# Two visits of small products made one: scores and sums of a head pair as one block inside an MLP unit

## The chip, the cores and the metric

The kernel runs on one core of one Trainium2 chip. The metric is the device time of one execution in microseconds; the kernel before takes 1026.38 us (median of three runs, 1025.25 to 1026.70). The five engines of the core are called as the profile calls them: PE is TensorE (PEld its weight loads), DVE is VectorE, ACT is ScalarE, POOL is GpSimd, SP is SyncE, which here only issues transfers.

## The reference

Retention (attention with a decay in place of a softmax), followed by an MLP with a PReLU. All of it is float32; `rel` is the distance of the positions, row minus column. Eight batches of eight heads, 576 positions, head dimension 64; the MLP has 4608 tokens, model width 512 and hidden width 2048.

```python
scores = scale * np.matmul(q, k.transpose(0, 1, 3, 2))      
gamma = 1.0 - 2.0 ** (-5.0 - np.arange(H, dtype=np.float32))
Dmat = np.where(rel >= 0, gamma[:, None, None] ** rel[None, :, :], 0.0)
attn_out = np.matmul(scores * Dmat[None, :, :, :], v)
x = attn_out.transpose(0, 2, 1, 3).reshape(B * S, H * D)
h = x @ w_in
g = np.maximum(h, 0.0) + alpha * np.minimum(h, 0.0)
out = g @ w_out
```

## The kernel before, in words

**Attention.** The kernel works on pairs of heads: number n of `pairs` is batch n // 4, heads 2c and 2c+1 with c = n % 4. The 576 positions are nine chunks (j) of 64. Inside a chunk the masked product of scores and values is computed directly. What earlier chunks give is carried in a running sum of 64x64 matrices. A pair goes through these steps:

- `load_pair`: twelve transfers bring kx and qx (blocks of 32 for the transposes), kn and vn. Two buffers of each, so a pair can be loaded while the one before it is in use.
- `scale_pair`: GpSimd multiplies qx by a table (L524), ScalarE scales vn by the decay (L529).
- `transposes`: VectorE turns qx and kx into qT and kT (L535). There is one buffer of each, and the running sums su share the buffer of kT.
- `pair_scores`: 18 products of 64x64 on TensorE (L552) into two PSUM tiles, even and odd chunks; ScalarE copies qT into mt (L555); four VectorE instructions scale and mask the scores into mt (L560).
- `pair_states`: 16 products of 64x64 (L571) into two PSUM tiles of the same pool (`ps_a`, two banks); ScalarE copies the even ones to su (L576), seven VectorE instructions form the running sums (L578, L582, L584). `pair_sums`: ScalarE copies them behind the values in vn (L590).
- `pair_values`: 18 products 128 deep and 64 wide (L601), and copies into the block of MLP input xb (L610).

A 64x64 product uses a quarter of the array[...]. The two heads and the even and odd chunks are laid out so that four products in a row use the four quarters.

**MLP.** Tokens go in 18 blocks (kb) of 256. From block 2 on each layer is a seven-product scheme in place of eight (sums of inputs and weights are made beforehand: `combine_x` on GpSimd, L449). A block is eight units (i). `mlp_unit` makes 14 products of the first layer (L463) into two PSUM tiles ph[0] and ph[1], one buffer each; ph[0] has four slots of 128 columns, of which three are used. ScalarE copies one slot (L469); VectorE adds the others (L474), applies the PReLU (L477, L479) and makes the sums for the second layer (L485), in the tile g. Then `mlp_out` makes the 14 records, seven products, of the second layer (L381) for the unit **before** this one, whose g is ready by then. With a block's last unit, seven VectorE instructions and two transfers write the output (L367, L368, L371).

**What sets the order.** Batches 0 and 1 and the first two token blocks are written out by hand. After `ordered.close()` a scheduler of the framework orders each engine's instructions from the order of the program and its own costs; each engine then runs them strictly in that order, and semaphores hold it where data is missing. The loop at L892 feeds it: for each pair of batches 2 to 7 (24 pairs) it writes the scores, then a third of the pair's share of MLP units, then the sums, a third, then the scaling and transposing of the next pair and the values, and the last third. A batch has 16 units to share out (24 for batch 4). 24 more units follow the last pair.

Of the kernel before, what the change touches and what calls it, by code (L numbers as in the profile page):

```python
# [18 lines left out]
def kernel(  # L19
# [49 lines left out]
    def half(x):  # L69
        return slice(x * C, (x + 1) * C)  # L70
# [36 lines left out]
    def load_pair(n):  # L107
        b, c = pairs[n]
        kx, qx, kn = [nat.tile([P, S], FP32, tag=t, name=f"{t}_{n}") for t in ("kx", "qx", "kn")]
        kx, qx = [t.rearrange("p (n r) -> p n r", r=32) for t in (kx, qx)]  # L110
        kn = kn.rearrange("p (j d) -> p j d", d=D)
        vn = nat.tile([P, 2, NJ, D], FP32, tag="vn", name=f"vn_{n}")
        load_sq(kx, k, b, c)
        load_sq(qx, q, b, c)
        for t, src in ((vn, v), (kn, k)):
            for h2 in range(2):
                load_head(t[half(1 - h2), h2] if t is vn else t[half(1 - h2)], src, b, 2 * c + h2)
        for h2 in range(2):

            nc.scalar.copy(vn[half(h2), h2, 0], zero[half(h2)])  # L120
        return kn, kx, qx, vn
# [326 lines left out]
                          (t[:, 2], b21, t[:, 1])):  # L448
            nc.gpsimd.tensor_tensor(out=o, in0=x0, in1=x1, op=ALU.subtract)  # L449

    def mlp_unit(kb, i):
        if kb not in xt:
            combine_x(kb)
        x, t = xb[kb], xt[kb]
        ph = [ps_h.tile([P, 4, P], FP32, tag=f"psh{m}", name=f"ph{m}_{kb}_{i}")
              for m in range(2)]

        for n, (m, o, l, r) in enumerate((
                (0, 2, 0, x[:, 0:2, 0:P]), (0, 0, 2, x[:, 2:4, 0:P]), (0, 1, 5, t[:, 1]),
                (1, 0, 4, t[:, 0]), (1, 1, 1, x[:, 0:2, P:TB]),  # L460
                (1, 2, 6, x[:, 2:4, P:TB]), (1, 3, 3, t[:, 2]))):
            for cc in range(2):
                nc.tensor.matmul(ph[m][:, o], w_in[i // UST][:, l, i % UST, cc], r[:, cc],  # L463
                                 start=(n in (0, 3) and cc == 0), stop=(n in (2, 6) and cc == 1),
                                 skip_group_check=True)


        g = mlp.tile([P, 8, P], FP32, tag="g", name=f"g_{kb}_{i}")
        nc.scalar.copy(g[:, 7], ph[0][:, 2])  # L469
        for o, x0, x1 in ((g[:, 0:5:4], ph[0][:, 0:2], g[:, 7:8].to_broadcast([P, 2, P])),  # L470
                          (g[:, 5:7], ph[1][:, 0:2], g[:, 4:5].to_broadcast([P, 2, P])),
                          (g[:, 3], ph[1][:, 0], g[:, 6]),
                          (g[:, 1:3], ph[1][:, 2:4], g[:, 5:7])):
            nc.vector.tensor_tensor(out=o, in0=x0, in1=x1, op=ALU.add)  # L474
        for m in range(2):
            fc = m * NU + i
            nc.vector.tensor_scalar(g[:, 4 + 2 * m:6 + 2 * m], g[:, 2 * m:2 * m + 2], 0.0,  # L477
                                    alpha[:, fc:fc + 1], ALU.min, ALU.mult)
        nc.vector.scalar_tensor_tensor(  # L479
            out=g[:, 0:4].rearrange("p x t -> p (x t)"),  # L480
            in0=g[:, 0:4].rearrange("p x t -> p (x t)"), scalar=0.0,
            in1=g[:, 4:8].rearrange("p x t -> p (x t)"), op0=ALU.max, op1=ALU.add)
        for o, x0, x1, op in ((4, 1, 3, ALU.add), (6, 0, 1, ALU.subtract),
                              (5, 4, 0, ALU.subtract), (7, 2, 5, ALU.subtract)):
            ins = nc.vector.tensor_tensor(out=g[:, o, :], in0=g[:, x0, :], in1=g[:, x1, :], op=op)  # L485

        combine(3, ins)
        assert i < NU - UST or not waiting
        pend.append((kb, i, g))
        if len(pend) > 1:  # L490
            mlp_out()
# [14 lines left out]
    def pop_units(n):  # L506
        for _ in range(min(n, len(queue))):
            kb, i = queue.pop(0)
            mlp_unit(kb, i)
            if i == NU // 2 and kb + 1 < NKB and ready[kb + 1] <= done[0]:  # L510
                combine_x(kb + 1)

# [30 lines left out]
    def pair_scores(n, kT, qT):  # L543
        c = pairs[n][1]

        mt = attn.tile([P, 2 * S], FP32, tag="at", name=f"mt_{n}").rearrange(
            "p (h j s) -> p h j s", h=2, s=C)
        ps = [ps_tile([P, NM, C], f"ps{p2}_{n}") for p2 in range(2)]
        for j in range(NJ):
            for h2 in range(2):  # L550
                x = (1 - h2, h2)[j % 2]
                nc.tensor.matmul(ps[j % 2][half(x), j // 2], kT[half(h2), chunk(j)],  # L552
                                 qT[half(h2), chunk(j)], start=True, stop=True)
        for h2 in range(2):
            nc.scalar.copy(mt[half(h2), h2].rearrange("p j s -> p (j s)"), qT[half(h2)])  # L555
        for p2 in range(2):
            for h2 in range(2):
                h, to, x = 2 * c + h2, half(1 - h2), (1 - h2, h2)[p2]
                nm = NM - p2
                nc.vector.scalar_tensor_tensor(  # L560
                    out=mt[to, h2, p2::2], in0=ps[p2][half(x), 0:nm], scalar=th[to, 3, h:h + 1],
                    in1=mask[to, None, :].to_broadcast([C, nm, C]), op0=ALU.mult, op1=ALU.mult)
        return mt

    def pair_states(n, kn, vn):
        c = pairs[n][1]
        ps = [ps_tile([P, NM - 1, D], f"pu{p2}_{n}") for p2 in range(2)]
        for j in range(NJ - 1):
            for h2 in range(2):
                x = (h2, 1 - h2)[j % 2]  # L570
                nc.tensor.matmul(ps[j % 2][half(x), j // 2], kn[half(1 - h2), j],  # L571
                                 vn[half(1 - h2), h2, j], start=True, stop=True)
        su = attn.tile([P, S], FP32, tag="kT", name=f"su_{n}")[:, 0:S - D].rearrange(
            "p (j d) -> p j d", d=D)
        g1, g2 = gch[:, 0, c:c + 1], gch[:, 1, c:c + 1]
        nc.scalar.copy(su[:, 0::2], ps[0])  # L576
        for h2 in range(2):
            nc.vector.scalar_tensor_tensor(  # L578
                out=su[half(h2), 1::2], in0=su[half(h2), 0::2], scalar=g1[half(h2)],
                in1=ps[1][half(1 - h2)], op0=ALU.mult, op1=ALU.add)  # L580
# [3 lines left out]
        nc.vector.scalar_tensor_tensor(out=su[:, 2::2], in0=su[:, 1:NJ - 3:2], scalar=g1,  # L584
                                       in1=ps[0][:, 1:], op0=ALU.mult, op1=ALU.add)
        return su

    def pair_sums(vn, su):
        for h2 in range(2):
            nc.scalar.copy(vn[half(h2), h2, 1:], su[half(h2)])  # L590

    def pair_values(n, vn, mt):
        b, c = pairs[n]
# [295 lines left out]
    enqueue(0)  # L889
    enqueue(1)  # L890

    for n, (b, c) in enumerate(pairs):  # L892
        if n <= last:
            continue
        if n == last + 1:
            pop_units(1)
        if n + 1 < len(pairs) and n + 1 not in loaded:
            loaded[n + 1] = load_pair(n + 1)
        kn, _, _, vn = loaded[n]
        share = -(-len(queue) // (NPAIR - c))  # L900
        cuts = [(share + i) // 3 for i in range(3)][::-1]
        kT, qT = turned.pop(n)
        mt = pair_scores(n, kT, qT)
        pop_units(cuts[0])
        pair_sums(vn, pair_states(n, kn, vn))
        pop_units(cuts[1])
        if n + 1 < len(pairs):
            scale_pair(n + 1)
            turned[n + 1] = transposes(n + 1)
        pair_values(n, vn, mt)  # L910
        del loaded[n]
        pop_units(cuts[2])
        if c == NPAIR - 1:
            enqueue(b)
    pop_units(len(queue))
    while pend:
        mlp_out()
# [28 lines left out]
```

## Time and profile before

| what | measured |
|---|---|
| time, median of three | 1026.38 us |
| span of the profiled execution | 1024.3 us |
| PE busy, matmuls | 1008.2 us, 98% |
| DVE busy | 767.9 us, 75% |
| ACT busy | 268.8 us, 26% |
| POOL busy | 179.0 us, 17% |
| granted PE clock | 0.995 |
| L381, second layer | 1792 records, 407.8 us busy |
| L463, first layer | 3584 records, 491.1 us busy in two groups |
| L552, L571, L601, attention | 1008, 896 and 1008 records, 22.3, 19.4 and 35.5 us busy |

Busy time is what the records cover. Matmuls are pipelined, so a record is longer than the distance to the next one: to price work on TensorE, subtract the starts of neighbouring groups in the timeline. A float32 product leaves two records. A bracket at the end of a timeline line is idle time of the engine ahead of it, with what ended it; a line without one started with no gap.

### The profile page before, as it was taken

To read this page: it belongs to the slowest core of one execution; us is meant where nothing else is said; L and a number is where in the kernel's file an instruction comes from. 1 tells how busy PE (TensorE), PEld (TensorE's weight loads), DVE (VectorE), ACT (ScalarE), POOL (GpSimd) and SP (SyncE) were. 2 spreads that over 40 slices of the span, in tenths; PEclk is the share of its full clock that TensorE was granted. 3 is DMA by queue.
4 is the path that set the end of the run, shared out by engine and by line. 5 is a ranking of instruction groups with operands and counts; after the bars stand their busy time and mean duration, and the time that the engine had idled before them with its cause. 6 is when DMAs were issued, how large, how long until landed. Compare 5 with 4: busy or idle time off the path is not lost.

```text
span 1024.3 us, 23109 instructions
## 1 busy us (share of the span) xinstructions
PE 1008.2 (98%) x9385; PEld 890.8 (87%) x9385; DVE 767.9 (75%) x2038; ACT 268.8 (26%) x605; POOL 179.0 (17%) x201
## 2 busy tenths in 40 slices
PE   6999999999999999999999999999999999999998
PEld 5666668999999999999999999999999999999997
DVE  6769967787878787776868787877787777667665
ACT  4656652223222222122122221222222211000000
POOL 5656675200200010100010000200020001010000
PEclk8999999999999999999999999999999999999999
DMA  9985744223223222112113222222222100000000
GB/s 238 235 195 150 180 78 93 48 57 59 64 41 68 48 47 57 25 46 47 39 30 67 48 53 45 63 48 56 48 48 57 24 22 2 22 1 21 1 21 22
DMA packets 229307, 64.30 MB, mean 63 GB/s; under 512 B 214336, under 2 KB 222544, under 8 KB 229200
## 3 DMA queue, kind: packets, MB, share of 16 engines
q1 hardware_dynamic: 227088, 62.29, 26.8%
q8 instruction: 74, 1.21, 0.5%
q10 hardware_dynamic: 2112, 0.53, 0.3%
q14 instruction: 33, 0.27, 0.1%
HBM read 53.35 MB, written 9.44 MB: 61 GB/s over the span
## 4 chain that ended last, share of the span: by engine, by line
PE 97%; SPq 1%; DVE 1%; ACT 0%; DMA 0%; issue 0%; DVEq 0%
PE ph L463 40%; PE po L381 38%; PE ph L419 6%; PE po L398 6%; PE pv L601 3%; PE ps L552 2%; PE pu L571 2%; SPq L78 1%; DMA raw<-in_moe_w_in_dram 0%; PE pv L720 0%; DVE wc L310 0%; DVE wc L307 0%; ACT wa L296 0%; ACT raw L298 0%; PE pv L709 0%
## 5 line engine op out<-in xcount | busy, mean ns | idle before, releaser
L381 PE MATMUL po<-w_out,g 128*128 128x256 f32 x1792 | 407.8, 379 | 0.0
L381 PEld LDWEIGHTS po<-w_out,g 128*128 128x128 f32 x1792 | 330.9, 190 | 39.6
L474 DVE TENSOR_TENSOR g<-ph,g 128x256 f32<-128x256 f32 (+1 forms) x512 | 187.9, 388 | 184.4 <-ACT g L469 112.6
L463 PE MATMUL ph<-xb,w_in 128*128 128x128 f32 x2048 | 277.7, 279 | 0.0
L463 PEld LDWEIGHTS ph<-xb,w_in 128*128 128x128 f32 x2048 | 253.2, 192 | 8.2 <-issue 0.5
L463 PE MATMUL ph<-xt,w_in 128*128 128x128 f32 x1536 | 213.4, 275 | 0.0
L463 PEld LDWEIGHTS ph<-xt,w_in 128*128 128x128 f32 x1536 | 192.1, 192 | 0.0
L469 ACT COPY g<-ph 128x128 f32<-128x128 f32 x128 | 33.9, 265 | 394.9 <-PE ph L463 372.9
L485 DVE TENSOR_TENSOR g<-g 128x128 f32<-128x128 f32 x512 | 126.9, 289 | 7.8
L479 DVE SCALAR_TENSOR_TENSOR g<-g 128x512 f32<-128x512 f32 x128 | 91.7, 717 | 3.9
L477 DVE TENSOR_SCALAR g<-g,alpha 128x256 f32<-128x256 f32 x256 | 85.0, 374 | 3.7
L524 POOL TENSOR_TENSOR qx<-qx,tabx 128x576 f32<-128x576 f32 x28 | 32.9, 1174 | 310.2 <-DMA qx<-in_q_dram 264.0
L419 PE MATMUL ph<-xb,w_in 128*128 128x256 f32 x256 | 61.1, 394 | 0.7 <-POOL w_out L697 0.7
L560 DVE SCALAR_TENSOR_TENSOR mt<-ps,th,mask 64x320 f32<-64x320 f32 (+1 forms) x112 | 57.8, 516 | 4.5 <-PE ps L552 2.6
L398 PE MATMUL po<-w_out,g 128*128 128x512 f32 x128 | 58.6, 599 | 0.9 <-DVE g L435 0.9
L419 PEld LDWEIGHTS ph<-xb,w_in 128*128 128x128 f32 x256 | 49.7, 197 | 10.7 <-issue 2.4
L449 POOL TENSOR_TENSOR xt<-xb 128x256 f32<-128x256 f32 x16 | 11.6, 727 | 214.6 <-PE ph L463 202.4
L449 POOL TENSOR_TENSOR xt<-xb,xt 128x256 f32<-128x256 f32 x32 | 23.6, 736 | 142.6 <-ACT xb L610 141.9
L529 ACT ACTIVATE vn<-vn,tabv 64x576 f32<-64x576 f32 x56 | 43.3, 773 | 16.7 <-DMA vn<-in_v_dram 15.9
L398 PEld LDWEIGHTS po<-w_out,g 128*128 128x128 f32 x128 | 23.4, 190 | 24.5 <-issue 21.8
L590 ACT COPY vn<-su 64x512 f32<-64x512 f32 x56 | 34.5, 616 | 37.8 <-DVE su L584 37.2
L610 ACT COPY xb<-pv 128x256 f32<-128x256 f32 (+3 forms) x84 | 22.6, 321 | 78.8 <-PE pv L601 78.7
(122 smaller groups left out, 688.5 us busy)
## 6 DMA issues: line engine op xcount, KB each, us to landing
out_dram<-osb SPq DMA_DIRECT2D x36, 256.0 KB, 2.3
kx<-in_k_dram SPq DMA_DIRECT2D x112, 72.0 KB, 2.7
qx<-in_q_dram SPq DMA_DIRECT2D x112, 72.0 KB, 2.4
vn<-in_v_dram SPq DMA_DIRECT2D x56, 144.0 KB, 3.2
kn<-in_k_dram SPq DMA_DIRECT2D x56, 144.0 KB, 3.2
raw<-in_moe_w_in_dram SPq DMA_DIRECT2D x24, 256.0 KB, 4.4
raw<-in_moe_w_out_dram SPq DMA_DIRECT2D x10, 512.0 KB, 5.2
w_in<-in_moe_w_out_dram SPq DMA_DIRECT2D x6, 512.0 KB, 5.1
```

Of the source, the lines that this page charges most:

```text
L381: nc.tensor.matmul(acc[kb][n // 2][:, n % 2, :], g[:, x, :], w_out[i][:, y, :], start=(i == 0 and n % 2 == 0), stop=(i == NU - 1 and (n % ...
L398: nc.tensor.matmul(acc[kb][m], g[:, 2 * x + m], w_out[i][:, 2 * x:2 * x + 2].rearrange("p x f -> p (x f)"), start=(i == 0 and x == 0), sto ...
L419: nc.tensor.matmul(ph[:, x], w_in[i // UST][:, cc // 2 * 2 + x, i % UST, cc % 2], xb[kb][:, cc], start=(cc == 0 and x == 0), stop=(cc == N ...
L449: nc.gpsimd.tensor_tensor(out=o, in0=x0, in1=x1, op=ALU.subtract)
L463: nc.tensor.matmul(ph[m][:, o], w_in[i // UST][:, l, i % UST, cc], r[:, cc], start=(n in (0, 3) and cc == 0), stop=(n in (2, 6) and cc == ...
L474: nc.vector.tensor_tensor(out=o, in0=x0, in1=x1, op=ALU.add)
L477: nc.vector.tensor_scalar(g[:, 4 + 2 * m:6 + 2 * m], g[:, 2 * m:2 * m + 2], 0.0, alpha[:, fc:fc + 1], ALU.min, ALU.mult)
L479: nc.vector.scalar_tensor_tensor(out=g[:, 0:4].rearrange("p x t -> p (x t)"), in0=g[:, 0:4].rearrange("p x t -> p (x t)"), scalar=0.0, in1 ...
L485: ins = nc.vector.tensor_tensor(out=g[:, o, :], in0=g[:, x0, :], in1=g[:, x1, :], op=op)
L529: nc.scalar.activation(vn[x, h2], vn[x, h2], ACTF.Copy, scale=tabv[x, c:c + 1])
L560: nc.vector.scalar_tensor_tensor(out=mt[to, h2, p2::2], in0=ps[p2][half(x), 0:nm], scalar=th[to, 3, h:h + 1], in1=mask[to, None, :].to_bro ...
L590: nc.scalar.copy(vn[half(h2), h2, 1:], su[half(h2)])
```

## The change

Before, TensorE leaves the MLP's 128x128 products three times for each pair: for the scores, the sums and the values, each between an L381 and an L463. After it, scores and sums are one block of 34 products of 64x64, placed inside a unit, behind its L463 products and ahead of L381. To have room for both in the two banks of `ps_a`, each tile now holds eight scores and eight sums, and the ninth score (chunk j=8) goes into the unused fourth slot of ph[0]. Its two small masks (64x64) are written directly behind the block, the four big ones after the unit's work on g, the running sums after the following unit, and the values with the next pair's scaling and transposes after the one behind that. The units that take a block are chosen so that none is a block's first or last unit: mostly the second and fifth.

```diff
-    def mlp_unit(kb, i):
+    def mlp_unit(kb, i, front=None):
...
+        rest = front(ph[0][:, 3]) if front else None
...
         combine(3, ins)
         assert i < NU - UST or not waiting
+        if rest:
+            rest()
         pend.append((kb, i, g))
...
+    def pair_front(n, kT, qT, kn, vn):
...
+        def products(extra):
+            ps = [ps_tile([P, 2, NM - 1, C], f"ps{p2}_{n}") for p2 in range(2)]
+            for j in (NJ - 1, *range(NJ - 1)):
+                for h2 in range(2):
+                    x = half((1 - h2, h2)[j % 2])
+                    nc.tensor.matmul(extra[x, 0:C] if j == NJ - 1 else ps[j % 2][x, 0, j // 2],
+                                     kT[half(h2), chunk(j)], qT[half(h2), chunk(j)],
+                                     start=True, stop=True, skip_group_check=True)
+            for j in range(NJ - 1):
+                for h2 in range(2):
+                    x = half((h2, 1 - h2)[j % 2])
+                    nc.tensor.matmul(ps[j % 2][x, 1, j // 2], kn[half(1 - h2), j],
+                                     vn[half(1 - h2), h2, j], start=True, stop=True,
+                                     skip_group_check=True)
+            for h2 in range(2):
+                to = half(1 - h2)
+                nc.vector.scalar_tensor_tensor(
+                    out=mt[to, h2, NJ - 1], in0=extra[to, 0:C],
+                    scalar=th[to, 3, 2 * c + h2:2 * c + h2 + 1], in1=mask[to],
+                    op0=ALU.mult, op1=ALU.mult)
+
+            def rest():
+                for h2 in range(2):
+                    nc.scalar.copy(mt[half(h2), h2].rearrange("p j s -> p (j s)"), qT[half(h2)])
+                for p2 in range(2):
+                    for h2 in range(2):
+                        h, to, x = 2 * c + h2, half(1 - h2), (1 - h2, h2)[p2]
+                        nc.vector.scalar_tensor_tensor(
+                            out=mt[to, h2, p2:NJ - 1:2], in0=ps[p2][half(x), 0],
+                            scalar=th[to, 3, h:h + 1],
+                            in1=mask[to, None, :].to_broadcast([C, NM - 1, C]),
+                            op0=ALU.mult, op1=ALU.mult)
+                later.append(lambda: pair_sums(vn, running_sums(n, ps[0][:, 1], ps[1][:, 1])))
...
+        for u in range(nq):
+            front = None
+            if u in begin:
+                n = begin[u]
+                if n + 1 < len(pairs) and n + 1 not in loaded:
+                    loaded[n + 1] = load_pair(n + 1)
+                front = pair_front(n, *turned.pop(n), loaded[n][0], loaded[n][3])
+            pop_units(1, front)
+            if u - 1 in begin:
+                later.pop(0)()
+            if u - 2 in begin:
+                n = begin[u - 2]
+                if n + 1 < len(pairs):
+                    scale_pair(n + 1)
+                    turned[n + 1] = transposes(n + 1)
+                pair_values(n, loaded[n][3], mts.pop(n))
+                del loaded[n]
```

More of the change, by code (lines that the diff above doesn't have):

```diff
@@ L504, in enqueue, with pop_units @@
                 queue.extend((kb, i) for i in range(NU))
-    def pop_units(n):
+    def pop_units(n, front=None):
         for _ in range(min(n, len(queue))):
             kb, i = queue.pop(0)
-            mlp_unit(kb, i)
+            mlp_unit(kb, i, front)
             if i == NU // 2 and kb + 1 < NKB and ready[kb + 1] <= done[0]:
@@ L565, in pair_states @@
     def pair_states(n, kn, vn):
-        c = pairs[n][1]
         ps = [ps_tile([P, NM - 1, D], f"pu{p2}_{n}") for p2 in range(2)]
@@ L572, in pair_states, with running_sums @@
                                  vn[half(1 - h2), h2, j], start=True, stop=True)
+        return running_sums(n, *ps)
+    def running_sums(n, even, odd):
+        c = pairs[n][1]
         su = attn.tile([P, S], FP32, tag="kT", name=f"su_{n}")[:, 0:S - D].rearrange(
@@ L575, in pair_states @@
         g1, g2 = gch[:, 0, c:c + 1], gch[:, 1, c:c + 1]
-        nc.scalar.copy(su[:, 0::2], ps[0])
+        nc.scalar.copy(su[:, 0::2], even)
         for h2 in range(2):
@@ L579, in pair_states @@
                 out=su[half(h2), 1::2], in0=su[half(h2), 0::2], scalar=g1[half(h2)],
-                in1=ps[1][half(1 - h2)], op0=ALU.mult, op1=ALU.add)
+                in1=odd[half(1 - h2)], op0=ALU.mult, op1=ALU.add)
         for j in range(3, NJ - 1, 2):
@@ L584, in pair_states @@
         nc.vector.scalar_tensor_tensor(out=su[:, 2::2], in0=su[:, 1:NJ - 3:2], scalar=g1,
-                                       in1=ps[0][:, 1:], op0=ALU.mult, op1=ALU.add)
+                                       in1=even[:, 1:], op0=ALU.mult, op1=ALU.add)
         return su
@@ L590, in pair_sums @@
             nc.scalar.copy(vn[half(h2), h2, 1:], su[half(h2)])
+    later = []
+    def pair_front(n, kT, qT, kn, vn):
+        c = pairs[n][1]
+        mts[n] = mt = attn.tile([P, 2 * S], FP32, tag="at", name=f"mt_{n}").rearrange(
+            "p (h j s) -> p h j s", h=2, s=C)
+        assert C == D and NJ == 9
+        def products(extra):
[30 more added lines that the diff above has]
+                later.append(lambda: pair_sums(vn, running_sums(n, ps[0][:, 1], ps[1][:, 1])))
+            return rest
+        return products
     def pair_values(n, vn, mt):
@@ L890 @@
     enqueue(1)
[L892 to L914, printed above, removed]
+    for b in range(2, B):
+        nq, first, at = len(queue), b * NPAIR, {}
+        for c in range(NPAIR):
+            u = c * nq // NPAIR
+            while queue[u][1] in (0, NU - 1):
+                u += 1
+            assert u + 2 < nq and (not at or at[c - 1] + 2 < u)
+            at[c] = u
+        begin = {u: first + c for c, u in at.items()}
+        for u in range(nq):
[15 more added lines that the diff above has]
+                del loaded[n]
+        enqueue(b)
     pop_units(len(queue))
```

## The prediction

> **What bounds the kernel now.** I read the page's busy table and chain of waits first: is one engine the bound, and does it ever wait?
>
> ```profile
> PE 1008.2 (98%) x9385; PEld 890.8 (87%) x9385; DVE 767.9 (75%) x2038; ACT 268.8 (26%) x605; POOL 179.0 (17%) x201
> ...
> PE 97%; SPq 1%; DVE 1%; ACT 0%; DMA 0%; issue 0%; DVEq 0%
> ```
>
> The chain that ended last is TensorE for 97%. Then the timeline of TensorE in the middle (start, length, line, tile shape, records; one f32 product is two records):
>
> ```profile
> 505.77 3.19 PE L381 MATMUL po<-w_out,g 128*128 128x256 f32 x14
> 508.89 0.69 PE L571 MATMUL pu<-vn,kn 64*64 64x64 f32 x32
> 509.52 1.16 PE L463 MATMUL ph<-xb,w_in 128*128 128x128 f32 x8
> ...
> 512.75 3.19 PE L381 MATMUL po<-w_out,g 128*128 128x256 f32 x14
> 515.77 1.05 PE L463 MATMUL ph<-xb,w_in 128*128 128x128 f32 x8
> ...
> 518.89 3.19 PE L381 MATMUL po<-w_out,g 128*128 128x256 f32 x14
> 522.01 1.27 PE L601 MATMUL pv<-mt,vn 128*64 128x64 f32 x36
> 523.21 1.16 PE L463 MATMUL ph<-xb,w_in 128*128 128x128 f32 x8
> ...
> 532.59 3.19 PE L381 MATMUL po<-w_out,g 128*128 128x256 f32 x14
> 535.70 0.80 PE L552 MATMUL ps<-qT,kT 64*64 64x64 f32 x36
> 536.43 1.16 PE L463 MATMUL ph<-xb,w_in 128*128 128x128 f32 x8
> ...
> 539.66 3.19 PE L381 MATMUL po<-w_out,g 128*128 128x256 f32 x14
> ```
>
> No line has a bracket of idle time: TensorE is packed. Subtract starts. With nothing in between, L381 holds the array 515.77-512.75 = 3.02 us, and L463 518.89-515.77 = 3.12. Ahead of the sums block (L571) L381 holds it 3.12, and behind it L463 holds it 512.75-509.52 = 3.23. So a block of small products costs its own span (sums 0.63, scores 0.73, values 1.20) plus 0.10 at the neighbour ahead and 0.10 at the one behind. All 24 later pairs read so, within 0.01 us; no unit shows a stall. Time can only leave or enter through TensorE.
>
> How much of a small block is fixed? Blocks of the first stage answer:
>
> ```profile
> 33.01 1.11 PE L681 MATMUL pu<-w_out,w_out 64*64 64x64 f32 x64
> 34.06 3.72 PE L419 MATMUL ph<-xb,w_in 128*128 128x256 f32 x16
> ...
> 45.50 0.68 PE L745 MATMUL ps<-w_out 64*64 64x64 f32 x16
> 46.11 7.17 PE L419 MATMUL ph<-xb,w_in 128*128 128x256 f32 x32
> ```
>
> L745 has 8 products and takes 0.61; L571 has 16 and takes 0.63; L681 has 32 and takes 1.05. Time does not follow the number of products but the rounds on the busiest 64x64 quarter of the array: L745 uses two quarters (4 rounds each), L571 four (4 rounds), L681 four (8 rounds), the scores four (18 products: 5 rounds on two quarters). From scores and sums: one round = 0.728-0.625 = 0.103 (24-pair means), fixed part = 0.625-4x0.103 = 0.213. It gives 0.63 for L745 and 1.04 for L681: it holds.
>
> **What the Trainium skill says.** "TensorEngine Tiling (Array Packing)", Key Properties: a change of tiling mode drains TensorE, while tiles of one mode run independently. The trace agrees: 0.2 us fixed in the block and 0.2 at its neighbours, at each visit. "TensorE: Matmul & The Clock Gate", The mechanism: products start and end in program order; so a product whose quarter is busy holds up those behind it. "GPSIMD Engine Reference", 1. Specifications: GpSimd shares SBUF interfaces with VectorE, in contention with instructions that have two SBUF inputs or the 2-port mode. The trace agrees, and it matters below; VectorE, once without and once with GpSimd's L449 running (532.83 to 535.82):
>
> ```profile
> 507.09 0.62 DVE L477 TENSOR_SCALAR g<-g,alpha 128x256 f32<-128x256 f32 x2
> 507.75 0.69 DVE L479 SCALAR_TENSOR_TENSOR g<-g 128x512 f32<-128x512 f32 x1
> ...
> 533.90 1.34 DVE L477 TENSOR_SCALAR g<-g,alpha 128x256 f32<-128x256 f32 x2
> 535.28 1.09 DVE L479 SCALAR_TENSOR_TENSOR g<-g 128x512 f32<-128x512 f32 x1
> ```
>
> They lose 0.72 and 0.40 us. L474, which reads PSUM, keeps its 1.08 for three.
>
> **TensorE's part of the change.** Removed, in each of the 24 pairs of batches 2 to 7: two visits, (0.728+0.20)+(0.625+0.20) = 1.753 us. Added: one visit of the same 34 products between L463 and L381. In the ordered stage before 150 us the scores block stood twice between L419 and L398, in that direction: also 0.73 plus 0.10 on each side, so the place costs nothing. Rounds of the merged block: scores j=8 comes first, on the same two quarters as j=0 behind it, then quarters alternate: 5 rounds of scores and 4 of sums on the busier pair, 9x0.103+0.213 = 1.14. At the seam the order of the two quarters turns round. The first stage has such a seam: L661 and L681 take 2.03 together where 16 rounds give 1.86. So the seam costs 0 to 0.17; I take 0.05, as one quarter waits there for a fraction of a round. Block 1.19, visit 1.39, gain 1.753-1.39 = 0.36 a pair, 24 x 0.36 = 8.7 us. Ends: seam 0 gives 9.9; seam 0.17 gives 5.8; if nothing but the neighbours' 0.20 were saved, 4.8.
>
> Values blocks (L601), the number of MLP units, the first 150 us and the 24 units after the last pair are the same.
>
> **VectorE's part.** Two masks of 64x320 become 64x256 and two of 64x64 are added: L560's forms (550 and 482 ns) differ by 68 ns for 64 elements, so 64x64 is some 0.28; 24x(2x0.28-2x0.07) = +10 us of busy time, on an engine idle for a quarter of the time. What matters is when. In the changed program's order VectorE does, in the front unit: two small masks, L474's first form, the next pair's qT transpose, then the other L474s and L477, L479 with the four big masks between, the four L485 with one sum; in the next unit L474 to L485 with the other sums and the kT transpose. I lay that out from t=0 at the block's first product, with distances between starts as the trace has them (mask 0.46, L474 0.33 to 0.38, transpose 0.68, L477 0.30, L479 0.70, L485 0.26, sums 0.50 and 0.26).
>
> New wait: the small masks need the block's first products, some 0.4; ScalarE's L469 now waits for them (they read the same bank), 0.93 to 1.27, behind which L474 and everything of this unit queue on VectorE. L474 ends at 3.9, L479 at 6.0, the third L485 at 7.3. TensorE needs the ph banks at 1.4+3.1 = 4.5 (the first; its reader is done at 1.7) and 5.8 (the second), and g at 7.6 (L479) and 8.4 (third L485): met by 1 to 2 us. Next unit: it starts late, at 8.1; L474 ends at 10.8 against 11.9, L479 at 12.5 against 13.7, the third L485 at 14.0 against 14.6. Smallest margin 0.5 us. The unit after has nothing extra and catches up. So I cost VectorE at nothing, hidden by L381's 3 us and L463's 3.1 us. The danger: GpSimd scales qx (1.15 us) about 4.8 us after qT is transposed (498.9 to 503.7 in the trace), or later by 1.6 where two kn loads stand ahead, so at 7 to 10: beside L485 and the SBUF sums. At the rate above it may take 0.3 to 0.5 us, the whole margin.
>
> Hidden and costed at nothing: vn and kn loads (issued a pair ahead, landing in 3.2 us), ScalarE's copies (26% busy; the sums reach vn some 4 us before the values need them), PSUM buffers of the pair (values copied out 0.6 us after they end, 3 us before the next block).
>
> **The rivals.**
> - A, VectorE's chain becomes a wait in part: margin 0.5 eaten, TensorE waits 0.1 to 0.3 at a pair. For: the margin, and GpSimd's turn falls there. Against: my lag is an estimate on the late side. 24x0.2 = 4.8: 1017.7+4.8 = 1022.5.
> - B, nothing gained: a block's time is 0.052 a product, whatever the visits (34x0.052 = 1.75, the old sum). For: scores and sums alone fit it. Against: L745 and L681 don't. 1026.4.
> - C, slower: GpSimd's turn costs the full 1.1 us seen above, 0.6 beyond the margin, and the front's late L469 adds 0.1: 24x0.7 = 16.8 lost for 8.7: 1034.5. Against: it needs every qx scaling to hit SBUF-only instructions from end to end.
>
> **How the numbers follow.** Forecast 0.68, A 0.19, B 0.05, C 0.08. Time 1026.4-8.7 = 1017.7. The range goes from 1015.3 (9.9, and 24 x 0.05 for half a round less in the block) to 1023.5, which takes in the seam at its dearest and A's middle, and leaves out B, C. Faster by over 0.2% (below 1024.3): forecast and nearly all of A, 0.86; within: 0.06; slower: 0.08.
>
> **What the profile after would show.** L614 and L620 (the changed kernel's scores and sums) one behind the other, 1.14 to 1.3 us together, 24 times; 3.22 for the L463 ahead and 3.12 for the L381 behind. L381 and L463 elsewhere still 3.02 and 3.12 without a bracket: then VectorE is hidden. A bracket at L463 or L381 "<-DVE g" in the unit behind a front would be rival A or C; a merged block near 1.55 with no brackets, rival B. Wrong I would be if the quarters of scores and sums don't overlap as one stream.

## The result and the profile after

The changed kernel takes 1019.69 us (median of six runs, 1017.73 to 1021.92), the kernel before, on the same chip, 1026.13 (1025.25 to 1026.86): a ratio of 0.9937, interval 0.9923 to 0.9951. It is faster by 6.4 us; the forecast was 1017.7, 8.7 us faster. So the question is what became of 2 us.

In the changed kernel L469, L474, L477, L479, L485 have become L471, L476, L479, L481, L487; L524 is L528, L535 is L539, L582 (sums of two SBUF inputs) is L589, L601 is L656. The scores are L614, the sums L620. The page's busy table and its chain of waits:

```profile
PE 1001.3 (98%) x9385; PEld 894.2 (88%) x9385; DVE 778.3 (76%) x2086; ACT 269.4 (26%) x605; POOL 179.2 (18%) x201
...
PE 94%; DVE 3%; DMA 1%; ACT 0%; issue 0%; SPq 0%; POOL 0%; DVEq 0%; ACTq 0%
```

VectorE's busy time rose by 10.4 us, and its share of the chain from 1% to 3%: TensorE now waits for it somewhere. The timeline of TensorE in the middle of the run, a pair's block and what is round it:

```profile
497.57 0.27 PE L614 MATMUL ph<-qT,kT 64*64 64x64 f32 x2
...
498.16 0.68 PE L620 MATMUL ps<-vn,kn 64*64 64x64 f32 x31
498.77 3.29 PE L381 MATMUL po<-w_out,g 128*128 128x256 f32 x14
501.89 1.05 PE L463 MATMUL ph<-xb,w_in 128*128 128x128 f32 x8
...
505.02 3.19 PE L381 MATMUL po<-w_out,g 128*128 128x256 f32 x14
508.04 1.05 PE L463 MATMUL ph<-xb,w_in 128*128 128x128 f32 x8
...
511.17 3.19 PE L381 MATMUL po<-w_out,g 128*128 128x256 f32 x14
514.28 1.27 PE L656 MATMUL pv<-mt,vn 128*64 128x64 f32 x36
```

Subtract starts: the merged block is 498.77 - 497.57 = 1.20 us (1.19 or 1.20 in all 24 pairs), L381 behind it 3.12, the next L463 3.13, the next L381 3.02: no wait here. The same view of the first pair of batch 2 reads otherwise:

```profile
171.17 3.19 PE L381 MATMUL po<-w_out,g 128*128 128x256 f32 x14
174.19 1.05 PE L463 MATMUL ph<-xb,w_in 128*128 128x128 f32 x8
175.09 0.61 PE L463 MATMUL ph<-xt,w_in 128*128 128x128 f32 x4
176.38 0.68 PE L463 MATMUL ph<-xt,w_in 128*128 128x128 f32 x4 [0.68 <-DVE g L476]
176.90 1.06 PE L463 MATMUL ph<-xb,w_in 128*128 128x128 f32 x8
177.79 0.61 PE L463 MATMUL ph<-xt,w_in 128*128 128x128 f32 x4
178.24 3.54 PE L381 MATMUL po<-w_out,g 128*128 128x256 f32 x14
181.70 1.27 PE L656 MATMUL pv<-mt,vn 128*64 128x64 f32 x36
```

The unit's L463 takes 178.24 - 174.19 = 4.05 us in place of 3.12, and L381 3.46 in place of 3.12. The second pair (L463 at 196.69, L381 at 200.10) loses another 0.28 and 0.34. With 0.08 of trifles that is 1.97 us of waiting, all but those trifles in two of 24 pairs.

I use one more number for each run below: the *stretch* from the first L463 of the trace to TensorE's last record, which leaves the first 150 us out. It is 866.04 us before and 859.42 after, 6.62 less. In it, the blocks give 3.80, their neighbours 4.80, and the waits take 1.97 back: 8.60 - 1.97 = 6.63.

What VectorE and GpSimd did at the first of those waits, from the timeline of all engines:

```profile
171.66 3.96 POOL L324 TENSOR_TENSOR w_in<-w_in 128x512 f32<-128x512 f32 x3 [4.78 <-DVE g L487]
172.00 0.48 DVE L585 SCALAR_TENSOR_TENSOR su<-su,gch,ps 64x256 f32<-64x256 f32 x1
172.51 1.84 DVE L589 SCALAR_TENSOR_TENSOR su<-su,gch 128x64 f32<-128x64 f32 x2
...
174.28 0.41 DVE L476 TENSOR_TENSOR g<-ph,g 128x256 f32<-128x256 f32 x1
174.61 1.09 DVE L589 SCALAR_TENSOR_TENSOR su<-su,gch 128x64 f32<-128x64 f32 x1
...
175.62 0.61 DVE L476 TENSOR_TENSOR g<-ph,g 128x128 f32<-128x128 f32 x2
```

GpSimd makes the last sums of weights (L324, three instructions of 1.27 us), and beside them three L589 take 1.84 + 1.09 = 2.93 us (one alone takes 0.28, as a run below shows). The L476 behind them are late by as much, and they empty the PSUM bank that L463 wants at 175.70. The instructions that read PSUM (L585 0.48, L476 0.41) are as long as ever.

### The profile page after: what moved, and what is told of

It reads as the page before. It is cut to its first block, busy times and chain, and to the rows that moved or that the text cites. A ratio compares the mean times of both kernels' runs of the same rounds, so it can differ in the third digit from the quotient of the medians.

```text
span 1018.5 us, 23084 instructions
## 1 busy us (share of the span) xinstructions
PE 1001.3 (98%) x9385; PEld 894.2 (88%) x9385; DVE 778.3 (76%) x2086; ACT 269.4 (26%) x605; POOL 179.2 (18%) x201
## 4 chain that ended last, share of the span: by engine, by line
PE 94%; DVE 3%; DMA 1%; ACT 0%; issue 0%; SPq 0%; POOL 0%; DVEq 0%; ACTq 0%
PE ph L463 38%; PE po L381 37%; PE ph L419 6%; PE po L398 6%; PE pv L656 3%; PE ps L614 1%; PE ps L620 1%; DMA w_out<-in_k_dram 1%; PE ph L614 1%; DVE su L589 0%; DVE g L476 0%; PE pt L697 0%; DVE mt L636 0%; PE ps L716 0%; PE ps L556 0%
## 5 line engine op out<-in xcount | busy, mean ns | idle before, releaser
L381 PE MATMUL po<-w_out,g 128*128 128x256 f32 x1792 | 410.9, 381 | 0.2
L381 PEld LDWEIGHTS po<-w_out,g 128*128 128x128 f32 x1792 | 330.1, 190 | 42.7 <-DVE g L487 1.3
L476 DVE TENSOR_TENSOR g<-ph,g 128x256 f32<-128x256 f32 (+1 forms) x512 | 187.0, 386 | 127.2 <-ACT g L471 75.2
L463 PE MATMUL ph<-xb,w_in 128*128 128x128 f32 x2048 | 272.7, 276 | 0.0
L463 PEld LDWEIGHTS ph<-xb,w_in 128*128 128x128 f32 x2048 | 257.1, 192 | 7.9 <-issue 0.7
L463 PE MATMUL ph<-xt,w_in 128*128 128x128 f32 x1536 | 213.8, 275 | 0.7 <-DVE g L476 0.7
L463 PEld LDWEIGHTS ph<-xt,w_in 128*128 128x128 f32 x1536 | 192.2, 192 | 1.1 <-PE ph L463 0.8
L487 DVE TENSOR_TENSOR g<-g 128x128 f32<-128x128 f32 x512 | 127.2, 289 | 5.4
L471 ACT COPY g<-ph 128x128 f32<-128x128 f32 x128 | 34.1, 266 | 327.7 <-PE ph L463 217.1
L528 POOL TENSOR_TENSOR qx<-qx,tabx 128x576 f32<-128x576 f32 x28 | 32.3, 1153 | 379.6 <-DMA qx<-in_q_dram 223.4
L481 DVE SCALAR_TENSOR_TENSOR g<-g 128x512 f32<-128x512 f32 x128 | 91.3, 714 | 3.8
L479 DVE TENSOR_SCALAR g<-g,alpha 128x256 f32<-128x256 f32 x256 | 84.3, 370 | 2.8
L419 PEld LDWEIGHTS ph<-xb,w_in 128*128 128x128 f32 x256 | 50.1, 198 | 11.0 <-issue 2.4
L625 DVE SCALAR_TENSOR_TENSOR mt<-ph,th,mask 64x64 f32<-64x64 f32 x48 | 13.6, 283 | 52.5 <-PE ph L614 52.2
L636 DVE SCALAR_TENSOR_TENSOR mt<-ps,th,mask 64x256 f32<-64x256 f32 x96 | 46.1, 481 | 2.3
L589 DVE SCALAR_TENSOR_TENSOR su<-su,gch 128x64 f32<-128x64 f32 x84 | 43.1, 513 | 2.1
```

What stands on the lines that cost most here:

```text
L381: nc.tensor.matmul(acc[kb][n // 2][:, n % 2, :], g[:, x, :], w_out[i][:, y, :], start=(i == 0 and n % 2 == 0), stop=(i == NU - 1 and (n % ...
L419: nc.tensor.matmul(ph[:, x], w_in[i // UST][:, cc // 2 * 2 + x, i % UST, cc % 2], xb[kb][:, cc], start=(cc == 0 and x == 0), stop=(cc == N ...
L481: nc.vector.scalar_tensor_tensor(out=g[:, 0:4].rearrange("p x t -> p (x t)"), in0=g[:, 0:4].rearrange("p x t -> p (x t)"), scalar=0.0, in1 ...
L636: nc.vector.scalar_tensor_tensor(out=mt[to, h2, p2:NJ - 1:2], in0=ps[p2][half(x), 0], scalar=th[to, 3, h:h + 1], in1=mask[to, None, :].to_ ...
```

## The experiments

All medians; each ratio is against the kernel before, measured beside it (1025.94 to 1026.34). Theory: the gain is two visits made one, and the missing 2 us are GpSimd's doing.

**The visit by itself.** The sums' block goes between the unit's products for ph[0] and those for ph[1], the scores stay behind the unit's L463: two visits again, everything else as changed.

```diff
+            if n == 3 and front:
+                front = front()
...
         rest = front(ph[0][:, 3]) if front else None
```

> The changed kernel, but the 16 sums products stand between the first layer's products into ph[0] and those into ph[1], and the scores behind them as in the change: two visits in place of one, with the same products, tiles, masks and units. Theory (each visit to 64x64 products costs 0.2 us at its neighbours and 0.21 us of start and end in the block, the products themselves cost 0.103 us a round): sums block 0.63, scores block 0.73, 0.10 at each of the four neighbours, so 0.35 us more a pair and 24 x 0.35 = 8.4 us more than the changed kernel: about 1028. Rival (a product costs 0.052 us however it is grouped, and the change gained by its place or by its order on VectorE): no change against the changed kernel, 1019.7 within 1 us.

Measured: 1025.36 us, ratio 0.9994 (0.9986 to 1.0003); stretch 866.12. The gain is gone. In its timeline of TensorE:

```profile
496.13 0.61 PE L465 MATMUL ph<-xt,w_in 128*128 128x128 f32 x4
496.67 0.69 PE L616 MATMUL ps<-vn,kn 64*64 64x64 f32 x32
497.29 0.71 PE L465 MATMUL ph<-xt,w_in 128*128 128x128 f32 x4
497.84 1.06 PE L465 MATMUL ph<-xb,w_in 128*128 128x128 f32 x8
498.73 0.61 PE L465 MATMUL ph<-xt,w_in 128*128 128x128 f32 x4
499.27 0.27 PE L625 MATMUL ph<-qT,kT 64*64 64x64 f32 x2
```

The four records of L465 ahead of each block hold the array 0.54 us (496.67 - 496.13), and the four behind the sums 0.55, where undisturbed ones hold it 0.45: 0.10 on each side, as before. Sums 0.62, scores 0.73. That is 24 x 0.353 = 8.5 us more than the merged block, less the 1.8 of waits that this order of VectorE didn't have: 6.7, as the stretch says. The time is near what the theory forecast and far from an unchanged one.

**The place.** The whole block between the products of ph[0] and ph[1].

```diff
+            if n == 3:
+                rest = front(ph[0][:, 3]) if front else None
...
-        rest = front(ph[0][:, 3]) if front else None
```

> The changed kernel, but the whole block of 34 products stands between the first layer's products into ph[0] and those into ph[1], some 1.8 us earlier in the unit. Theory (place costs TensorE nothing; what is left of loss is VectorE being late in the unit behind): block 1.20 and 0.10 at each neighbour as in the change, VectorE gets the masks 1.8 us earlier, so the two stalls shrink from 1.9 us to under 0.5: 1018 to 1019.7. Rival (the place behind all of L463 is what makes the block cheap, for instance because only there the array is drained anyway): neighbours cost more, 0.1 to 0.2 us a pair, 1022 to 1025.

Measured: 1016.90 us, ratio 0.9910 (0.9897 to 0.9924); stretch 857.60.

```profile
492.62 0.27 PE L613 MATMUL ph<-qT,kT 64*64 64x64 f32 x2
...
493.82 0.71 PE L465 MATMUL ph<-xt,w_in 128*128 128x128 f32 x4
```

The block stays at 493.82 - 492.62 = 1.20 us (1.19 or 1.20 in all pairs) with 0.10 on each side: a place inside the unit costs nothing. The waits are gone too. The masks start earlier, VectorE's order is another, and in the first pair of batch 2 the three sums (L588 here) are done before GpSimd begins the weights' sums:

```profile
168.58 0.28 DVE L588 SCALAR_TENSOR_TENSOR su<-su,gch 128x64 f32<-128x64 f32 x1
...
170.14 3.96 POOL L324 TENSOR_TENSOR w_in<-w_in 128x512 f32<-128x512 f32 x3 [3.81 <-PE ph L465]
```

**The seam.** The two heads of each chunk of the sums in the other order, so that the quarters keep their order across the seam.

```diff
             for j in range(NJ - 1):
-                for h2 in range(2):
+                for h2 in (1, 0):
```

> The changed kernel, but the two heads of each sums chunk are issued in the other order, so that at the seam between scores and sums the quarters of the array come in the same order as before. Theory (the measured 1.20 us of the merged block is 9 rounds of 0.103 and 0.21 fixed, 1.14, and the rest is the turned order at the seam): block 1.14 to 1.15, 24 x 0.05 = 1.2 us less than the changed kernel, about 1018.5. Rival (the rest comes from the ninth chunk and the first standing one behind the other on the same quarters, or the round is longer in a long block): block stays at 1.20, no change in time.

Measured: 1019.21 us, 0.9935 (0.9922 to 0.9947); the block is 1.19 to 1.20 as before. The order of quarters at the seam costs nothing; that part of the theory falls.

**Strict alternation.** Scores 0 to 8, sums 1, 0, 3, 2, 5, 4, 7, 6.

```diff
-            for j in (NJ - 1, *range(NJ - 1)):
+            for j in range(NJ):
...
-            for j in range(NJ - 1):
+            for j in (1, 0, 3, 2, 5, 4, 7, 6):
```

> The changed kernel with the scores in the order 0 to 8 and the sums in the order 1, 0, 3, 2, 5, 4, 7, 6, so that the two pairs of quarters alternate strictly from the first product to the last. Theory (the 0.05 of the merged block above 9 rounds comes from scores 8 and 0 one behind the other on the same quarters): block 1.14, 24 x 0.05 = 1.2 us less than the changed kernel, 1018.5. Rival (a round is simply 0.11 in a block this long): block 1.20, 1019.7. The small masks start 0.5 us later, since chunk 8 comes in the middle of the block, and VectorE's order changes; brackets of idle time at the MLP's products are counted apart.

Measured: 1016.91 us, 0.9907 (0.9883 to 0.9931); stretch 857.49. The block is again 1.20, so the theory of neighbours on the same quarters falls too, although the time is even below what it forecast: the waits went. Why is worth a look, for GpSimd's L324 stands where it stood:

```profile
171.31 4.09 POOL L324 TENSOR_TENSOR w_in<-w_in 128x512 f32<-128x512 f32 x3 [5.45 <-DVE g L487]
171.71 0.42 DVE L476 TENSOR_TENSOR g<-ph,g 128x256 f32<-128x256 f32 x1
172.06 0.61 DVE L589 SCALAR_TENSOR_TENSOR su<-su,gch 128x64 f32<-128x64 f32 x1
172.59 0.61 DVE L476 TENSOR_TENSOR g<-ph,g 128x128 f32<-128x128 f32 x2
173.12 0.90 DVE L589 SCALAR_TENSOR_TENSOR su<-su,gch 128x64 f32<-128x64 f32 x1
```

VectorE loses about as much (the three sums some 0.9 us, and the two L479 behind them another 1.0), but here the last L476, which free the bank, come ahead of the second L589, and the kT transpose (0.78) comes behind the four L487 in place of ahead of them. The later mask of chunk 8 had probably moved the scheduler's order. So a wait needs both: a sum that is held up, and work that TensorE wants queued behind it.

**Twice the sums.** The sums' 16 products issued twice, so that the block has 13 rounds on the busier quarters.

```diff
-            for j in range(NJ - 1):
+            for j in (*range(NJ - 1), *range(NJ - 1)):
```

> The changed kernel with the 16 products of the sums issued twice in the block (the second time the same values into the same place): 13 rounds on the busier quarters, all four in use. Theory with the prediction's round of 0.103 us (the 0.06 that the block has above 9 such rounds and the fixed 0.213 is a constant): block 1.20 + 4 x 0.103 = 1.61, 24 x 0.41 = 9.9 us more on TensorE, 1029.6 less what waits go away. Rival (a round is 0.110 in a long block): 1.64. Second rival (0.035 us a product, whatever the quarters, as 8 products between 0.63 and 1.20 could be read): 1.20 + 16 x 0.035 = 1.76, 1033.

Measured: 1034.39 us, 1.0084 (1.0070 to 1.0098). The block:

```profile
503.85 0.27 PE L614 MATMUL ph<-qT,kT 64*64 64x64 f32 x2
...
504.44 1.15 PE L620 MATMUL ps<-vn,kn 64*64 64x64 f32 x63
505.51 3.29 PE L381 MATMUL po<-w_out,g 128*128 128x256 f32 x14
```

505.51 - 503.85 = 1.66 us: four more rounds for 0.466, 0.117 each, above both forecasts by rounds and below the one by products. With 0.63 for four rounds and 1.20 for nine, a round is 0.114 and the fixed part 0.17, and 0.17 + 13 x 0.114 = 1.65: within 0.01, one line goes through all three. The block gives 24 x 0.466 = 11.2 us; the other 4.5 of the stretch's 15.7 are waits for g, 0.1 to 0.5 us in most pairs that have one. VectorE's order was another in this run.

**The same products, badly ordered.** The sums as chunks 0, 2, 4, 6, then 1, 3, 5, 7: 34 products as in the changed kernel.

```diff
-            for j in range(NJ - 1):
+            for j in (0, 2, 4, 6, 1, 3, 5, 7):
```

> The changed kernel with the 16 products of the sums in another order: chunks 0, 2, 4, 6, then 1, 3, 5, 7, so that eight products in a row use one pair of quarters and the next eight the other. Theory (a block's time is the rounds on the quarters, and a product whose quarter is busy holds up those behind it): 9 rounds on the first pair, then 4 more on the second, 13 rounds, 13 x 0.103 + 0.213 = 1.55 us in place of 1.19, 24 x 0.36 = 8.7 us on the 1019.7 of the changed kernel, so 1028. Rival (the time is 0.035 us a product plus a fixed part, whatever the quarters): the block stays at 1.20 and the time at 1019.7.

Measured: 1025.95 us, 0.9997 (0.9989 to 1.0005); stretch 865.95. The whole gain is gone, with not a product more:

```profile
500.18 0.27 PE L614 MATMUL ph<-qT,kT 64*64 64x64 f32 x2
...
500.81 0.93 PE L620 MATMUL ps<-vn,kn 64*64 64x64 f32 x32
501.68 3.29 PE L381 MATMUL po<-w_out,g 128*128 128x256 f32 x14
```

501.68 - 500.18 = 1.50 us. "A time per product" is refuted. 1.50 is less than the 1.55 expected, and 11.7 rounds of 0.114 where 13 were counted. An overlap where the two runs of eight meet would explain it; no run isolates that. The Trainium skill's "TensorE: Matmul & The Clock Gate", The mechanism (products start in program order) agrees with 1.50 against 1.20: the eight products for the idle pair of quarters stood behind eight for the busy one.

One rival is left. Even chunks also write one PSUM tile and odd chunks the other, so this run reorders the tiles together with the quarters. Chunk 8 speaks for the quarters. In the merged block it writes a third tile (ph[0]), yet it costs what it cost in the tile of the even chunks: 1.195 - 0.625 - 4 x 0.117 = 0.10 us here, 0.728 - 0.625 = 0.10 before.

**GpSimd moved away.** The weights' last sums not in units with a block, and five at a time in the others.

```diff
-        combine(3, ins)
+        combine(0 if front else 5, ins)
```

> The changed kernel, but GpSimd's last weight sums (L324) follow only units without a block of small products, five at a time in place of three, so that none runs beside the running sums of the next unit. Theory (the stalls of TensorE at 174 to 179 and 196 to 200 us, 1.9 us in the trace, come from VectorE's sums L589 taking 0.92 us in place of 0.30 beside L324): both stalls vanish, L589 there at 0.3 to 0.6 us, 1.9 us less than the changed kernel, about 1017.8. Rival (these two pairs are late for another reason, such as the first loads): the stalls stay, no change in time.

Measured: 1016.74 us, 0.9910 (0.9896 to 0.9923); stretch 857.78. VectorE's instructions come in the same order as in the changed kernel, and both waits in batch 2 are gone. VectorE and GpSimd at the first pair:

```profile
169.49 0.60 DVE L589 SCALAR_TENSOR_TENSOR su<-su,gch 128x64 f32<-128x64 f32 x2
...
170.34 0.28 DVE L589 SCALAR_TENSOR_TENSOR su<-su,gch 128x64 f32<-128x64 f32 x1
...
174.68 1.27 POOL L324 TENSOR_TENSOR w_in<-w_in 128x512 f32<-128x512 f32 x1 [10.73 <-DVE g L487]
```

The three L589 take 0.88 us in place of 2.93. What is left is 0.33 us of waits, in the L381 at 283.80 and 771.24.

**More work for VectorE.** The first two big masks written twice, 0.96 us a pair.

```diff
-                for p2 in range(2):
+                for p2 in (0, 0, 1):
```

> The changed kernel with the first two big masks of a pair written twice (the second time the same values into the same place): two more VectorE instructions of 0.48 us, 0.96 us a pair, within the unit that holds the block. Theory (VectorE's smallest margin behind the block is some 0.2 us, so VectorE isn't free there): about 0.7 us of waiting on TensorE a pair, with brackets at the MLP's products of the next unit, up to 24 x 0.7 = 17 us, so 1027 to 1037. Rival (the unit behind the block has 1 us to spare or more, as the prediction's 0.5 to 1.2 of most steps would have it if its smallest is not the one that counts): under 2 us more, 1020 to 1022.

Measured: 1018.70 us, 0.9923 (0.9903 to 0.9944); stretch 858.87. The rival's forecast, and even less time than the changed kernel. But the run doesn't measure the margin: the scheduler moved sums behind L476 and the kT transpose behind L487, and gave VectorE the room back.

**More work for GpSimd.** An extra sum (128x448) behind each scaling of qx; VectorE's order is unchanged.

```diff
+        if n >= 8:
+            junk = attn.tile([P, 448], FP32, tag="junk", name=f"junk_{n}")
+            q1 = qx.rearrange("p n r -> p (n r)")
+            nc.gpsimd.tensor_tensor(out=junk, in0=q1[:, 0:448], in1=q1[:, 0:448], op=ALU.add)
```

> The changed kernel with one more GpSimd instruction behind each scaling of qx: the sum of qx and qx (128x448), into a tile that nothing reads; its output isn't used. Theory (VectorE's waits come from GpSimd's instructions beside its sums, and VectorE has only some 0.2 us to spare behind a block): the extra 1 us of GpSimd falls beside the third L589, L591 or L479, which lose 0.3 to 0.7 us, so TensorE waits 0.1 to 0.5 us in most of the 24 pairs: 2 to 12 us more than the changed kernel, 1022 to 1032, with brackets at L463 and L381 in the middle of the run. Rival (only the weights' sums, 3.96 us long, matter; short GpSimd work is hidden): under 1 us more, 1019.7 to 1020.7, brackets as in the changed kernel, in batch 2 alone.

Measured: 1027.04 us, 1.0013 (1.0004 to 1.0023); stretch 867.96, 8.5 more than the changed kernel, for 22.4 us of work on an engine that is busy for 18% of the time. All engines, in the middle:

```profile
508.42 1.15 POOL L528 TENSOR_TENSOR qx<-qx,tabx 128x576 f32<-128x576 f32 x1 [25.88 <-DVE g L476]
508.83 1.82 DVE L593 SCALAR_TENSOR_TENSOR su<-su,gch 128x64 f32<-128x64 f32 x2
509.64 0.93 POOL L534 TENSOR_TENSOR junk<-qx 128x448 f32<-128x448 f32 x1
...
513.72 3.54 PE L381 MATMUL po<-w_out,g 128*128 128x256 f32 x14
...
514.83 2.02 PEld L381 LDWEIGHTS po<-w_out,g 128*128 128x128 f32 x10 [0.48 <-DVE g L487]
...
517.19 1.27 PE L660 MATMUL pv<-mt,vn 128*64 128x64 f32 x36
```

The two sums (L593 here) take 1.82 us. L381 holds the array 517.19 - 513.72 = 3.47 us in place of 3.12, as its weights wait 0.48 us for VectorE's g (L487): so in 19 of the 24 pairs. The danger that the prediction named at the scaling of qx is real; how much room the changed kernel has there is worked out below. The means of other instructions of VectorE hardly move (L487 292 ns against 289, the big masks 480 against 481).

**Does VectorE slow down, or stand still?** In the changed kernel 27 of these sums (L589) take over 0.33 us, and every one of them ends 0.08 us after an instruction of GpSimd does. Four others start before the GpSimd instruction that they meet, and keep their 0.28. The Trainium skill's "SBUF — State Buffer", SBUF: two separate sides, says that the port pair of GpSimd and VectorE is an exclusive lock, held for a whole instruction. If so, the price is what is left of the GpSimd instruction, and the same work in short pieces costs less. Two runs: the weights' sums behind a unit in pieces of 128 columns, and the extra sum of the last run in seven pieces of 64.

```diff
+            if after is None:
+                cut = [lambda k: w[:, k]]
+            elif len(w.shape) == 5:
+                cut = [lambda k, u=u, v=v: w[:, k, u, v] for u in range(UST) for v in range(2)]
+            else:
+                cut = [lambda k, m=m: w[:, k, m * P:(m + 1) * P] for m in range(HM // P)]
+            for f in cut:
+                ins = nc.gpsimd.tensor_tensor(out=f(o), in0=f(x), in1=f(y), op=op)
```

```diff
+            for m in range(0, 448, 64):
+                nc.gpsimd.tensor_tensor(out=junk[:, m:m + 64], in0=q1[:, m:m + 64],
+                                        in1=q1[:, m:m + 64], op=ALU.add)
```

> The changed kernel with the weights' sums that follow a unit cut into pieces of 128 columns on GpSimd (four or two instructions in place of one; 1.27 us for 128x512 and 0.73 for 128x256 before); VectorE's order is as in the changed kernel. There each L589 that meets GpSimd's work ends about 0.08 us after the GpSimd instruction does (172.51 + 0.49 = 173.00 against 172.93; 173.04 + 1.31 = 174.35 against 174.27; 174.61 + 1.09 = 175.70 against 175.62). Theory (such an instruction of VectorE stands still until GpSimd's instruction ends): each of the three L589 loses at most 0.4 us in place of 0.2, 1.0 and 0.8, so the brackets of 0.68 and 0.34 in batch 2 go or fall under 0.3 together: 1017.7 to 1018.3. Rival (the two engines share a rate, and VectorE loses by the time GpSimd is at work): the pieces are as long together or longer, the waits stay, 1019.7 or more.

> The run with the extra GpSimd sum behind each scaling of qx (1027.04 us), with that sum cut into seven instructions of 64 columns; its output isn't used; VectorE's order is as in the changed kernel. Theory (a sum of VectorE stands still until GpSimd's instruction ends): the second sum behind the block waits for a piece of some 0.2 us in place of 0.93, VectorE is some 0.5 us earlier in each pair, and the 17 waits of 0.34 us at L381 go: 1019.5 to 1022. Rival (a shared rate): the seven pieces together are as long as the one or longer, and the time stays at 1027 or goes up.

Measured: the pieces of the weights' sums 1017.68 us, 0.9917 (0.9905 to 0.9930), stretch 857.98; the pieces of the extra sum 1019.69 us, 0.9931 (0.9918 to 0.9945), stretch 860.74 against 867.96 in one piece. The weights' sums in pieces:

```profile
171.37 5.56 POOL L331 TENSOR_TENSOR w_in<-w_in 128x128 f32<-128x128 f32 x12 [4.80 <-DVE g L494]
172.23 0.92 DVE L596 SCALAR_TENSOR_TENSOR su<-su,gch 128x64 f32<-128x64 f32 x2
173.40 0.57 DVE L596 SCALAR_TENSOR_TENSOR su<-su,gch 128x64 f32<-128x64 f32 x1
```

and the extra sum in pieces:

```profile
509.41 1.15 POOL L528 TENSOR_TENSOR qx<-qx,tabx 128x576 f32<-128x576 f32 x1 [25.96 <-DVE g L476]
509.74 1.27 DVE L595 SCALAR_TENSOR_TENSOR su<-su,gch 128x64 f32<-128x64 f32 x2
```

GpSimd works longer in both (5.56 us against 3.96; seven pieces of the extra sum 1.80 against 0.93), and VectorE's sums lose less: 0.92 + 0.57 = 1.49 us for three in place of 2.93, and 1.27 for two in place of 1.82. By a shared rate both should have got worse. The page's lock agrees with these traces, and they show it for this form (two SBUF inputs), with 0.08 us from the end of one to the end of the other.

**How much room there is.** With GpSimd's work moved, added to or cut, VectorE's instructions keep the changed kernel's order, so one sum can be put to all these runs. In each pair, add up what the three L589 take beyond 0.28 us each; what exceeds 0.79 us is what TensorE waits. The 0.79 is read from the changed kernel. There the first pair loses 2.05 us and waits 1.27, the second loses 1.41 and waits 0.63, two more lose 0.82 and wait 0.04, and the other 20 lose at most 0.78 and wait for nothing. The other runs test it: over 24 pairs it gives 0.35 us with the weights' sums moved (0.33 measured), 10.05 with the extra sum (10.43), 3.12 with its pieces (3.27) and 0.43 with the weights' pieces (0.52).

**Both remedies.** The block between ph[0] and ph[1], and no weights' sums in its unit.

```diff
+            if n == 3:
+                rest = front(ph[0][:, 3]) if front else None
...
-        combine(3, ins)
+        combine(0 if front else 5, ins)
```

> The changed kernel with both edits that took the waits away: the block between the products of ph[0] and those of ph[1], and the sums of the weights made five at a time in units without a block and none in units with one. If both remove the same waits (1.98 us of brackets), the sum is no more than either alone: 1016.5 to 1017.0, 3 us below the changed kernel. If they remove different ones (the weights' sums the two long ones, the place those beside the scaling of qx), 1016.0 or less.

Measured: 1017.19 us, 0.9910 (0.9885 to 0.9935), stretch 857.55. That is a little above its forecast, and no better than either remedy alone: they remove the same waits. Either remedy alone, the strict alternation or both together end at 1016.7 to 1017.2, and their stretches at 857.5 to 857.8: the changed kernel's 859.42 less its 1.97 of waits is 857.45. Each beats both kernels by its median; their intervals overlap, so none is the best of them. With the changed kernel's interval theirs touch or overlap a little, so that they are faster than it by 1.6 to 1.9 us rests on the stretch.

## Why the prediction was right, and where 2 us went

- **TensorE never idles, so time leaves only through its visits: right.** Two visits at the old price were back at 1025.36.
- **Each visit costs 0.10 at the neighbour ahead and 0.10 behind: right.** L463 ahead of the block 3.22 (3.32 in ten cases, where a values block stands ahead of it too), L381 behind 3.13. The Trainium skill's "TensorEngine Tiling (Array Packing)", Key Properties, names a cause that fits (a change of tiling mode drains the array); the runs show the 0.10, not its cause. The neighbours gave 4.80 us, the forecast 24 x 0.20.
- **Block 1.19: right in size, wrong in its parts.** The step "9x0.103+0.213 = 1.14 ... I take 0.05" for the seam had too short a round. It was taken from scores minus sums, whose fifth round has two products, not four. The sums issued twice give the full round alone, 0.117 (0.466 / 4), and with the half-filled one at 0.103 the block comes out: 0.625 + 4 x 0.117 + 0.103 = 1.20. There is no seam. So that 1.19 was met is in part luck: a round taken too short, and a guess for a seam that isn't there. (The line above, 0.114 a round and 0.17 fixed, is the mean of both kinds.) The first stage's L661 and L681, which had suggested one, fit without: 0.17 + 16 x 0.114 = 1.99 against 2.03. L681 alone doesn't fit as well (1.08 against 1.05).
- **Order on the quarters decides: right.** The badly ordered block took 1.50 with the same products.
- **VectorE at nothing: the term that was mis-sized, 1.97 us in place of 0.** The layout itself held: in the pair at 497.57, counted from the block's first product, L476 stood at 1.35, L481 at 5.37, and the third L487 of the next unit ended at 14.2 (14.0 forecast), 0.63 of it lost by an L589 beside the scaling of qx. Two sizes were too small and offset each other. In 19 pairs GpSimd cost the sums 0.5 to 0.8 us, not 0.3 to 0.5, and the room was 0.79, not 0.5; that these pairs hardly waited is in part luck. What failed is "The danger: GpSimd scales qx". It named one piece of GpSimd's work and left out L324, which runs beside batch 2's first units and is in the trace of before too (three in 3.96 us at 167.85). And "At the rate above it may take 0.3 to 0.5 us" took a lock for a rate: beside one L324 of 1.27 us a sum stands still for up to 1.0, and three in a row are hit three times. The prediction's own lines hint at it: its slow L479 ends at 536.37, 0.55 us after the last L449 (535.82), which is less than the 0.69 that it takes alone.
- **Rival A had the right shape and the wrong place.** Waits for g came in two pairs, 1.27 and 0.63 us, not in 24 at 0.2. B falls with its time per product; C would have needed longer GpSimd work at each pair: with 0.93 us more of it, 1027.04 was measured.

The sum: 8.60 us through TensorE (8.7 forecast), 1.97 back through VectorE, 6.63; the stretch fell by 6.62, and the medians differ by 6.44. The forms of the changed kernel without waits, at 1016.7 to 1017.7, are where the forecast had put it.

## What to carry to other kernels

Small products on quarters of the array cost by visit and by round: put them together, and order them so that no long run of them uses the same quarters. When you lay out a second engine's work to see whether it stays hidden, list everything that a third engine runs in each stage, the early ones too, and price each meeting by the rest of the instruction it meets, not by a mean slow-down. Long GpSimd instructions beside VectorE's two-input SBUF work are best moved to another unit, or cut.

## What was not expected of the hardware

- VectorE's sums with two SBUF inputs, where GpSimd's instruction started first, end 0.08 us after the GpSimd instruction that they meet, whatever their own 0.28; cutting 0.93 us of GpSimd work into seven pieces gave back 7.2 us of the stretch although the work became longer.
- A round of four 64x64 float32 products takes 0.114 to 0.117 us, and a block some 0.17 on top, over 4, 9 and 13 rounds.
- When g came late, L381 lost 0.34 us again and again, and its weight load 0.48, although VectorE's delays differed (0.34 to 0.35 in 16 of the 24 pairs with the extra GpSimd sum); why the size repeats stays open.
